# Twelve slots of a hand-written plan changed in a fused attention and feed-forward kernel: transposes of x at other places, held stores behind loads, the last tile by eight block products

## The chip, the cores and the metric

The kernel runs on one core of a Trainium2 chip. Its time is the device time of one launch in microseconds (us), as the median of several runs. A profiled execution gives a trace of every instruction on the core's engines: TensorE (PE, with its weight loads as PEld), VectorE (DVE), ScalarE (ACT), GpSimd (POOL) and SyncE (SP), and of its DMA queues. "Busy" is time in which an engine executes an instruction that the profile counts, and the "span" reaches from the first to the last event of the trace.

## The reference

Cosine-weighted linear attention for 8 batches of 8 heads, 576 rows and 64 columns each, followed by a feed-forward network over all 8 × 576 = 4608 rows of 512 columns:

```python
def phi(x, c, s):
    r = np.maximum(x, 0.0)
    return np.concatenate([r * c, r * s], axis=-1)
q_p, k_p = phi(q, cos_w, sin_w), phi(k, cos_w, sin_w)      # 64 -> 128 columns
kv  = np.einsum('bhsf,bhsd->bhfd', k_p, v)
z   = np.sum(k_p, axis=2)
num = np.einsum('bhsf,bhfd->bhsd', q_p, kv)
den = np.einsum('bhsf,bhf->bhs', q_p, z)[..., None] + 1e-06
x   = (num / den) -> rows (batch, s), columns (head, d)     # 4608 x 512
a, b = x @ w1, x @ w2                                       # 512 -> 1024 columns each
out = ((a * b) @ w3) @ w_out                                # 1024 -> 1024 -> 512
```

## The kernel before

**Tiles and stages.** The feed-forward part works on nine tiles `t` = 0 to 8 of 512 rows of x, the attention on eight batches `b` = 0 to 7, each cut into five chunks `c` = 0 to 4 of 128, 128, 128, 128 and 64 rows. Early on, w3 and w_out are multiplied into one matrix of 1024 × 512 (`w34b`), so that each tile needs x·w1, x·w2, their product element by element, and one more product with `w34b`. A chunk goes through these steps:

- `k`, `q` (features): the cosine half on VectorE (L494), the sine half on ScalarE (L498); a third number in the plan says how many heads ScalarE takes, and VectorE takes the others (L501). `v` copies a chunk of v beside a column of ones (L513 on GpSimd; `V` and `A` give it to VectorE or ScalarE).
- `qd`: a DMA transpose of a chunk's q features into `qpT`, issued by SyncE (L521). Some early chunks are transposed on TensorE instead (`qt`, and `xt` for x).
- `kv`: the products of all chunks of a batch on TensorE (L548), then two casts into `kvs`, on ScalarE (L552) and VectorE (L553).
- `n`: numerator and denominator of one chunk on TensorE (L580), eight products of `qpT` with `kvs`.
- `d`: the division on VectorE, three instructions (L591 to L593), which write `xblk`.
- `xd`: a DMA transpose of `xblk` into a place of the tile's `xT`, issued by SyncE (L613). There are three `xT` buffers in turn.

The rows of a batch fall into tiles of 512 so that tile 5 needs x of chunks 2, 3, 4 of batch 4 and 4, 0 of batch 5, tile 6 those of 1, 2, 3 of batch 5 and 0 of batch 6, tile 7 those of 1 to 4 of batch 6 and 4 of batch 7, and tile 8 those of 0 to 3 of batch 7. A numerator `n b c` reads 128 columns of `qpT`; for the short chunk 4, of 64 rows, it reads 64 columns of a neighbour as well, so that `n 5 1` reads what `qd 5 1` wrote, and `n 7 4` what `qd 7 4` and `qd 7 0` wrote.

**Order.** The order is written out by hand as a text, `PLAN` (L26 to L259). Each line is a slot and each step in it a call; the calls issue their instructions in this order, and every engine executes its own instructions in that order. `f t` takes the next piece of tile `t` (the generator `ffn_groups`, L658): four matmuls of a w1 product into a PSUM bank and the cast `asb` on ScalarE (L708), then four of a w2 product and the multiplication `abT` on VectorE (L714), eight times over, and then the products with `w34b`. There are four such PSUM banks (`ffn_pool`), and two more from `more` on, late in tile 7.

**Seven or eight block products.** For tiles in the tuple `SEVEN` the product with `w34b` is made from seven products of 256-column blocks (`seven_products`, L776, with the matmuls at L794), with sums of the operands on VectorE (`sums`, L774, called at L716 to L721) and additions of the results (`add`, L802). For the last tile it differs: GpSimd takes two of the additions (`ON_POOL`), the last product is made in two halves (L843), and `out_now` stores each block as soon as it is there, on SyncE and ScalarE. A tile that is not in `SEVEN` takes plain products (L729): three blocks of 128 rows with eight matmuls of 512 columns each, copied by ScalarE, and in the last tile stored by SyncE at once; the fourth block of the last tile in two halves of eight matmuls with 256 columns, copied by ScalarE and VectorE and each stored at once (L742 to L750).

**Loads and stores.** GpSimd's queue issues the loads of q, k and v: `l` at its place; `lg` behind a small copy (`gate`, L418) that reads the newest `asb`, so that the load starts no sooner; `lt` behind the same copy of the newest transposed column, that is, of the transpose which the plan issued last. The results of tiles 0 to 6 are held (`held`) in pairs of 128-row blocks, 512 KB each, until the plan stores the oldest pair: `st` by GpSimd, `sg` by GpSimd behind the newest `asb`, `sx` by GpSimd behind the newest transpose, `ss` by SyncE. `gx 0` does nothing at this place. There are twelve result buffers (`osbs`), so tiles 6 and 7 write where tiles 0 and 1 had theirs.

**What the profile's lines are.** Transposes on SyncE's queue show as `DMA_TRANSPOSE` of L521 (qpT<-qp) and L613 (xT<-xblk); loads on GpSimd's as `DMA_DIRECT2D` of L375 to L388; stores as `DMA_DIRECT2D` of L652.

The gates and the two forms of stores behind them, as far as the change uses them:

```python
def gate(behind):
    nc.gpsimd.tensor_copy(out=seen[0:behind.shape[0]], in_=behind)
...
def gated_store():                      # sg
    gate(newest[0][:, 0:1])
    store_next()

def store_behind_transposes():          # sx
    gate(transposed[0])
    store_next()
```

Of the kernel before, what the change touches and what calls it, by code (L numbers as in the profile page):

```python
# [89 lines left out]
f 1; d 2 4; lt 4 k 0; d 2 3  # L90
f 1; kv 3
f 2; tw 2
f 2; lg 4 q 0
f 2
f 2; l 4 q 1; qd 3 1
f 2
f 2; lt 4 v 1; n 3 0; qd 3 4
f 2
f 2; qd 3 2; tw 3
f 2  # L100
f 2
f 2; d 3 0
f 2; xd 2 4; n 3 1
f 2; q 4 0; q 4 4; d 3 1
f 2; q 4 3; v 4 4 V; l 4 k 1; xd 3 1; n 3 4
f 2
f 2; d 3 4
f 2; q 4 1 0
f 2; xd 2 3; xd 3 0; k 4 1; k 4 0; xd 3 4; qd 4 3; n 3 2
f 2; l 5 v 0  # L110
f 2
f 2; q 4 2
# [12 lines left out]
f 3  # L125
f 3; n 4 0; k 5 4; n 4 1; d 4 0; l 6 v 1
f 3; v 5 3 V
f 3; d 4 1; v 5 4 V; xd 3 2; qd 4 4; xd 4 0
f 3
f 3; n 4 2; k 5 1; xd 4 1  # L130
f 3
# [1 line left out]
f 3  # L133
f 3; q 5 0
f 3; d 4 2; lt 6 q 0; q 5 4
f 3; xd 3 3; k 5 0; n 4 3; v 6 4 V; xd 4 2
f 3
f 3; k 5 3 4; k 5 2; v 5 1 V; lg 6 k 0; q 5 3
f 4
f 3; lt 7 k 0; d 4 3  # L140
f 4; q 5 2; qd 5 0
f 4; n 4 4
f 4
f 4; q 5 1 6; d 4 4; qd 5 4; v 6 1 G
f 4
f 4; qd 5 2; l 6 q 1; kv 5; xd 4 3
f 4
f 4; n 5 0; v 6 0 G
f 4
f 4; d 5 0  # L150
f 4; n 5 4; qd 5 3
f 4; d 5 4
f 4
f 4; lt 6 k 1
f 4; k 6 4; qd 5 1
f 4; lg 7 k 1
f 4
f 4; xd 4 4; xd 5 0; lt 7 v 0
f 4; v 6 2 A
f 4; q 6 4  # L160
f 4; k 6 0 2; q 6 2; n 5 3; k 6 1 6; xd 5 4; q 6 0 4
f 4
f 5
f 4; d 5 3; n 5 1; k 6 3 2; q 6 3
# [2 lines left out]
f 5  # L167
f 5; v 6 3 V
f 5; d 5 1; k 6 2 0
f 5; l 7 q 0; st  # L170
f 5
f 5
f 5; kv 6; sg; k 7 3 6; lt 7 q 1; qd 6 2
f 5; n 5 2; k 7 2; k 7 1; k 7 0 4; lg 7 v 1; qd 6 0
f 5; qd 6 4; xd 5 3; qd 6 3
f 5
# [9 lines left out]
f 5; n 6 2  # L186
f 5
f 6; v 7 3 V; n 6 3
f 6; qd 6 1; d 6 2; q 7 2
f 6; st; xd 6 2; gx 0  # L190
f 6; q 7 4 2
f 6; k 7 4; q 7 0
f 6; v 7 4 V
f 6; n 6 1; v 7 1 V
f 6; d 6 1; q 7 3 2
f 6; qd 7 2
f 6; d 6 3; qd 7 4; q 7 1
f 6
f 6; qd 7 3
f 6; qd 7 0; sg  # L200
f 6; qd 7 1; kv 7
f 6; n 7 4; xd 6 1
f 6; d 7 4; xd 6 3
f 6; xd 7 4
f 6
f 6
f 6
f 6
f 6
# [47 lines left out]
f 8  # L257
f 8
f 8"""  # L259
SEVEN = (2, 3, 4, 5, 6, 7, 8)  # L260
ON_POOL = (8,)
NKP, NVA, NQP, NRQ, NRV, NT3 = 1, 2, 1, 2, 2, 3

# [50 lines left out]
def kernel(  # L314
# [343 lines left out]
    def ffn_groups(t):  # L658
# [38 lines left out]

        seven = t in SEVEN
        s = [fsb.tile([P, 4, 256], BF16, name=f"s{i}", bufs=1) for i in range(3)] if seven else None
# [277 lines left out]
```

## Time and profile before

| what | value |
|---|---|
| runs | 250.39, 246.68 and 248.56 us, median 248.56 |
| profiled execution: its own time | 247.64 us |
| its span | 245.9 us, 5417 instructions |
| granted TensorE clock | 0.999 over the span |
| TensorE busy | 233.7 us, 95%, 2024 matmuls in the records |
| VectorE busy | 196.4 us, 80% |
| ScalarE busy | 110.8 us, 45% |
| GpSimd busy | 82.4 us, 34% |
| loads and stores by software queues (q0) | 23.60 MB, 65.6% of the 16 DMA engines' span |
| transposes and SyncE's stores (q1) | 16.13 MB, 40.9% |
| first product of tile 5, 6, 7, 8 | 154.02, 177.4, 200.0 and 221.0 us |
| last store lands | 244.81 us |

The times of parts are those of the one profiled execution, counted from its span's start; its own time holds 1.7 us that lie outside the span. In a list of waits a row gives the engine, the tile and line of the waiting instruction, what it waited for, and then the sum of these waits, their number and the longest, in us. In a list of instructions a row gives the start, the length, the engine and line, the operation with its tiles and shapes, and in brackets how long the engine had been idle ahead of it and for whom.

### The profile page before, as it was taken

How to read it: one execution, taken by the hardware profiler on the slowest of the kernel's cores; microseconds unless marked ns; L12 is line 12 of the kernel's file. 1: busy time of each engine (PE TensorE's matmuls, PEld its weight loads, DVE VectorE, ACT ScalarE, POOL GpSimd, SP SyncE). 2: the span in 40 equal slices, each digit the busy share in tenths (PEclk: the TensorE clock that was granted, in tenths of full speed). 3: DMA queues.
4: the chain of work that ended last, by engine and by line, in shares of the span. 5: the costliest groups of instructions: out<-in, count | busy, mean ns of one | idle time of the engine just before them, and what ended most of it. 6: DMA issues, size and time to landing. Idle time of an engine off the chain costs nothing.

```text
span 245.9 us, 5417 instructions
## 1 busy us (share of the span) xinstructions
PE 233.7 (95%) x2024; PEld 145.6 (59%) x2051; DVE 196.4 (80%) x466; ACT 110.8 (45%) x196; POOL 82.4 (34%) x153
## 2 busy tenths in 40 slices
PE   8899999989999999999999997999999999999992
PEld 2589544566964544765585556555855675484481
DVE  6776577968979847999989989789999688785662
ACT  2743323767654833835484346337174302313320
POOL 8653987633504070007112311325000100083012
PEclk9999999999999999999999999999999999999999
DMA  6999999999999999999999997999855952599925
GB/s 192 193 196 199 190 180 194 199 199 174 130 186 132 178 150 178 172 129 152 185 119 133 176 173 89 129 209 242 109 77 104 188 42 43 109 281 329 271 84 171
DMA packets 85322, 40.47 MB, mean 165 GB/s; under 512 B 48048, under 2 KB 82864, under 8 KB 85296
## 3 DMA queue, kind: packets, MB, share of 16 engines
q0 software_dynamic: 37616, 23.60, 65.6%
q1 hardware_dynamic: 47264, 16.13, 40.9%
q10 hardware_dynamic: 416, 0.39, 0.5%
q8 instruction: 16, 0.26, 0.5%
q14 instruction: 10, 0.08, 0.1%
HBM read 38.80 MB, written 9.44 MB: 196 GB/s over the span
## 4 chain that ended last, share of the span: by engine, by line
PE 66%; DMA 15%; DVE 7%; POOL 6%; issue 3%; SPq 1%; ACT 0%; DVEq 0%; POOLq 0%
PE ffnps L667 40%; PE ffnps L794 12%; PE ffnps L729 5%; DMA w2b<-in_moe_w_dram 4%; PE pnum L580 4%; DMA kf<-in_k_dram 3%; POOL early L406 3%; DMA qpT<-qp 3%; PE ffnmore L794 2%; DMA q<-in_q_dram 2%; PE pnum L548 2%; DMA xT<-xblk 2%; DVE qp L494 1%; DVE abT L714 1%; POOL early L412 1%
## 5 line engine op out<-in xcount | busy, mean ns | idle before, releaser
L667 PE MATMUL ffnps<-xT,w1b 128*128 128x512 bf16 (+2 forms) x338 | 74.4, 338 | 2.9 <-DMA xT<-xblk 2.0
L667 PE MATMUL ffnps<-xT,w2b 128*128 128x512 bf16 (+2 forms) x346 | 75.2, 339 | 0.4
L708 ACT CAST asb<-ffnps 128x512 bf16<-128x512 f32 x64 | 37.5, 585 | 78.3 <-PE ffnps L667 62.2
L714 DVE TENSOR_TENSOR abT<-asb,ffnps 128x512 bf16<-128x512 bf16 x64 | 43.5, 682 | 17.3 <-PE ffnps L667 17.1
L667 PEld LDWEIGHTS <-w1b 128*128 128x128 bf16 x352 | 31.6, 98 | 30.0 <-issue 3.0
L667 PEld LDWEIGHTS <-w2b 128*128 128x128 bf16 x352 | 31.4, 98 | 26.8
L593 DVE TENSOR_TENSOR xblk<-pnum,den 128x512 bf16<-128x512 f32 (+1 forms) x39 | 26.9, 691 | 1.3
L794 PEld LDWEIGHTS <-abT 128*128 128x128 bf16 x224 | 21.6, 98 | 3.7
L498 ACT ACTIVATE kp<-kf,sinv 128x512 bf16<-128x512 bf16 (+4 forms) x33 | 20.5, 655 | 2.9 <-DMA kf<-in_k_dram 2.8
L498 ACT ACTIVATE qp<-qs,sinv 128x512 bf16<-128x512 bf16 (+6 forms) x30 | 18.4, 626 | 3.3 <-DMA qs<-in_q_dram 1.7
L580 PEld LDWEIGHTS <-qpT 128*128 128x128 bf16 x320 | 15.0, 98 | 7.5 <-issue 1.9
L418 POOL COPY seen<-xT 128x1 bf16<-128x1 bf16 x6 | 1.2, 194 | 48.3 <-DMA xT<-xblk 48.3
L580 PE MATMUL pnum<-kvs,qpT 128*128 128x65 bf16 x312 | 16.3, 194 | 1.0 <-DMA qpT<-qp 0.5
L418 POOL COPY seen<-asb 128x1 bf16<-128x1 bf16 x13 | 3.0, 233 | 41.5 <-ACT asb L708 41.5
L794 PEld LDWEIGHTS <-s 128*128 128x128 bf16 x160 | 15.5, 98 | 2.2
L729 PE MATMUL ffnps<-w34b,abT 128*128 128x512 bf16 x60 | 14.9, 379 | 0.2
L494 DVE TENSOR_SCALAR kp<-kf,cosv 128x512 bf16<-128x512 bf16 (+1 forms) x40 | 14.4, 378 | 0.3 <-DMA kf<-in_k_dram 0.3
L794 PE MATMUL ffnps<-w34b,abT 128*128 128x256 bf16 x112 | 14.5, 273 | 0.1
L473 PE MATMUL ffnps<-early,w3T 128*128 128x512 bf16 x62 | 14.2, 379 | 0.1
L513 POOL COPY va<-vs 128x512 bf16<-128x512 bf16 (+1 forms) x13 | 8.5, 667 | 15.2 <-DMA vs<-in_v_dram 15.2
L494 DVE TENSOR_SCALAR qp<-qs,cosv 128x512 bf16<-128x512 bf16 (+1 forms) x35 | 13.2, 383 | 0.0
L794 PE MATMUL ffnps<-early,s 128*128 128x256 bf16 x96 | 11.6, 273 | 0.0
(129 smaller groups left out, 323.7 us busy)
## 6 DMA issues: line engine op xcount, KB each, us to landing
kf<-in_k_dram POOLq DMA_DIRECT2D x7, 320.0 KB, 7.8
early<-in_moe_w_dram POOLq DMA_DIRECT2D x16, 128.0 KB, 5.2
out_dram<-osb SPq DMA_DIRECT2D x8, 256.0 KB, 3.6
qs<-in_q_dram POOLq DMA_DIRECT2D x6, 320.0 KB, 7.0
vs<-in_v_dram POOLq DMA_DIRECT2D x6, 320.0 KB, 9.1
kf<-in_k_dram POOLq DMA_DIRECT2D x7, 256.0 KB, 8.7
qs<-in_q_dram POOLq DMA_DIRECT2D x6, 256.0 KB, 8.4
vs<-in_v_dram POOLq DMA_DIRECT2D x6, 256.0 KB, 10.1
```

The costliest lines, as they stand in the source:

```text
L406: nc.gpsimd.dma_start(out=w3b[ts(a, 32), ds(g0, n), :].rearrange("p g (c j) -> p (g c) j", c=4), in_=moe_w3[ds(128 * g0, 128 * n), ts(a, 2 ...
L473: nc.tensor.matmul(acc[:, :], lhsT=w3T[:, lc, :], rhs=woutb[:, lc, :], start=(lc == 0), stop=(lc == 7))
L494: nc.vector.tensor_scalar(out=dst[:R, c, :, 0:D], in0=rows[:R], scalar1=0.0, scalar2=cosv[:R, at:at + 1], op0=ALU.max, op1=ALU.mult)
L498: nc.scalar.activation(out=dst[:R, c, 0:n, D:F], in_=rows[:R, 0:n], func=ACTF.Relu, scale=sinv[:R, at:at + 1], bias=0.0)
L513: (copy or nc.gpsimd.tensor_copy)(out=att_of(b)["va"][:R, c, :, 0:D], in_=raw[b, "v"][:R, :, c, :])
L580: nc.tensor.matmul(nt[:, h // 4, ds((h % 4) * 65, 65)], lhsT=qpT[:, h, ds(at, 128)], rhs=kvs[:, h, :], start=True, stop=True)
L593: nc.vector.tensor_tensor(out=xblk[rows, g0:g0 + ng], in0=n4[:, :, :, 0:D], in1=den[rows, 0:ng].unsqueeze(3).to_broadcast([R, ng, 4, D]), ...
L667: nc.tensor.matmul(out, lhsT=w[:, kc, ts(jc, 128)], rhs=x[:, kc, tok], start=(kc == 0), stop=(kc == 3))
L708: nc.scalar.copy(out=asb[:], in_=aT[:, :])
L714: nc.vector.tensor_mul(out=abT[:, jc, :], in0=asb[:], in1=bT[:, :])
L729: nc.tensor.matmul(ops[:, :], lhsT=abT[:, jc, ts(ms, 128)], rhs=w34b[:, jc, :], start=(jc == 0), stop=(jc == 7))
L794: nc.tensor.matmul(into[:, ts(ms, 256)], lhsT=a[:, kc, ts(ms, 128)], rhs=b[:, kc, :], start=(ms == 0 and kc == 0), stop=(ms == 1 and kc == 3))
```

## The change

Only the plan's text and the tuple `SEVEN` change; no function does. By place:

- **Tiles 2 and 3 (slots of `f 2` and `f 3`).** `xd 2 3` is issued ahead of `qd 3 1`, `qd 3 4` and `qd 3 2` instead of late in `f 2`; the steps `d 3 0`, `xd 3 0`, `n 3 1`, `d 3 1`, `xd 3 1`, `n 3 4`, `d 3 4`, `xd 3 4` and the features of batch 4 between them stand one to eight slots sooner. `xd 3 3` goes ahead of `xd 4 0`.
- **`f 4`.** `q 5 2`, `q 5 1` and `d 4 4` stand one to three slots later (`q 5 1` behind `kv 5`). `xd 4 4`, `xd 5 0` and `xd 5 4`, which were three in a row behind `qd 5 1`, go in between: SyncE's order `qd 5 2`, `xd 4 3`, `qd 5 3`, `qd 5 1`, `xd 4 4`, `xd 5 0`, `xd 5 4` becomes `qd 5 2`, `xd 4 3`, `xd 4 4`, `qd 5 3`, `xd 5 0`, `xd 5 4`, `qd 5 1`. As `lt` waits for the transpose issued last, `lt 6 k 1` now reads the x of `xd 5 0` instead of the q of `qd 5 3`, and `lt 7 v 0` and `lt 7 q 1` follow other transposes too.
- **`f 5` and `f 6`, stores.** The first four held pairs (tiles 0 and 1) were stored by `st` and `sg` in `f 5` and by `st` and `sg` in `f 6`. Now all four stand in `f 6`: `sg` behind the first and second of its `asb`, and near its end `sx` (behind `xd 7 4`) and `st`.
- **`f 6`, attention.** `d 6 3`, `xd 6 3`, `n 6 1`, `d 6 1`, `xd 6 1`, `qd 7 4`, `qd 7 0` and `kv 7` stand sooner. SyncE's order from `xd 6 2` on, `qd 7 2`, `qd 7 4`, `qd 7 3`, `qd 7 0`, `qd 7 1`, `xd 6 1`, `xd 6 3`, `xd 7 4`, becomes `qd 7 4`, `xd 6 3`, `qd 7 0`, `xd 6 1`, `qd 7 2`, `qd 7 3`, `qd 7 1`, `xd 7 4`.
- **Tile 8.** It leaves `SEVEN`, and so takes the plain products: three blocks and two halves of one. Its sums, additions and stores from `seven_products` go.

```diff
@@ -90,23 +90,23 @@
 f 1; d 2 4; lt 4 k 0; d 2 3
 f 1; kv 3
 f 2; tw 2
-f 2; lg 4 q 0
+f 2; xd 2 3; lg 4 q 0
 f 2
 f 2; l 4 q 1; qd 3 1
 f 2
 f 2; lt 4 v 1; n 3 0; qd 3 4
 f 2
 f 2; qd 3 2; tw 3
+f 2; d 3 0
+f 2; xd 3 0; n 3 1
+f 2; d 3 1
+f 2; xd 2 4; xd 3 1
+f 2; q 4 0; q 4 4; n 3 4
+f 2; q 4 3; v 4 4 V; l 4 k 1
 f 2
-f 2
-f 2; d 3 0
-f 2; xd 2 4; n 3 1
-f 2; q 4 0; q 4 4; d 3 1
-f 2; q 4 3; v 4 4 V; l 4 k 1; xd 3 1; n 3 4
-f 2
-f 2; d 3 4
+f 2; d 3 4; xd 3 4
 f 2; q 4 1 0
-f 2; xd 2 3; xd 3 0; k 4 1; k 4 0; xd 3 4; qd 4 3; n 3 2
+f 2; k 4 1; k 4 0; qd 4 3; n 3 2
 f 2; l 5 v 0
 f 2
 f 2; q 4 2
@@ -125,7 +125,7 @@
 f 3
 f 3; n 4 0; k 5 4; n 4 1; d 4 0; l 6 v 1
 f 3; v 5 3 V
-f 3; d 4 1; v 5 4 V; xd 3 2; qd 4 4; xd 4 0
+f 3; d 4 1; v 5 4 V; xd 3 2; qd 4 4; xd 3 3; xd 4 0
 f 3
 f 3; n 4 2; k 5 1; xd 4 1
 f 3
@@ -133,32 +133,32 @@
 f 3
 f 3; q 5 0
 f 3; d 4 2; lt 6 q 0; q 5 4
-f 3; xd 3 3; k 5 0; n 4 3; v 6 4 V; xd 4 2
+f 3; k 5 0; n 4 3; v 6 4 V; xd 4 2
 f 3
 f 3; k 5 3 4; k 5 2; v 5 1 V; lg 6 k 0; q 5 3
 f 4
 f 3; lt 7 k 0; d 4 3
-f 4; q 5 2; qd 5 0
+f 4; qd 5 0
 f 4; n 4 4
-f 4
-f 4; q 5 1 6; d 4 4; qd 5 4; v 6 1 G
-f 4
+f 4; q 5 2
+f 4; qd 5 4; v 6 1 G
+f 4; d 4 4
 f 4; qd 5 2; l 6 q 1; kv 5; xd 4 3
-f 4
+f 4; xd 4 4; q 5 1 6
 f 4; n 5 0; v 6 0 G
 f 4
 f 4; d 5 0
 f 4; n 5 4; qd 5 3
-f 4; d 5 4
+f 4; d 5 4; xd 5 0
 f 4
-f 4; lt 6 k 1
+f 4; lt 6 k 1; xd 5 4
 f 4; k 6 4; qd 5 1
 f 4; lg 7 k 1
 f 4
-f 4; xd 4 4; xd 5 0; lt 7 v 0
+f 4; lt 7 v 0
 f 4; v 6 2 A
 f 4; q 6 4
-f 4; k 6 0 2; q 6 2; n 5 3; k 6 1 6; xd 5 4; q 6 0 4
+f 4; k 6 0 2; q 6 2; n 5 3; k 6 1 6; q 6 0 4
 f 4
 f 5
 f 4; d 5 3; n 5 1; k 6 3 2; q 6 3
@@ -167,10 +167,10 @@
 f 5
 f 5; v 6 3 V
 f 5; d 5 1; k 6 2 0
-f 5; l 7 q 0; st
-f 5
-f 5
-f 5; kv 6; sg; k 7 3 6; lt 7 q 1; qd 6 2
+f 5; l 7 q 0
+f 5
+f 5
+f 5; kv 6; k 7 3 6; lt 7 q 1; qd 6 2
 f 5; n 5 2; k 7 2; k 7 1; k 7 0 4; lg 7 v 1; qd 6 0
 f 5; qd 6 4; xd 5 3; qd 6 3
 f 5
@@ -186,24 +186,24 @@
 f 5; n 6 2
 f 5
 f 6; v 7 3 V; n 6 3
-f 6; qd 6 1; d 6 2; q 7 2
-f 6; st; xd 6 2; gx 0
-f 6; q 7 4 2
-f 6; k 7 4; q 7 0
-f 6; v 7 4 V
-f 6; n 6 1; v 7 1 V
-f 6; d 6 1; q 7 3 2
+f 6; qd 6 1; d 6 2; q 7 2; sg
+f 6; xd 6 2; gx 0; q 7 4 2
+f 6; d 6 3; sg; q 7 0
+f 6; qd 7 4; k 7 4; xd 6 3
+f 6; n 6 1; v 7 4 V
+f 6; d 6 1; v 7 1 V; qd 7 0
+f 6; q 7 3 2; xd 6 1
 f 6; qd 7 2
-f 6; d 6 3; qd 7 4; q 7 1
+f 6; q 7 1
 f 6
-f 6; qd 7 3
-f 6; qd 7 0; sg
-f 6; qd 7 1; kv 7
-f 6; n 7 4; xd 6 1
-f 6; d 7 4; xd 6 3
-f 6; xd 7 4
+f 6; qd 7 3; kv 7
 f 6
+f 6; qd 7 1
+f 6; n 7 4
+f 6; d 7 4; xd 7 4
 f 6
+f 6; sx
+f 6; st
 f 6
 f 6
 f 6
@@ -257,7 +257,7 @@
 f 8
 f 8
 f 8"""
-SEVEN = (2, 3, 4, 5, 6, 7, 8)
+SEVEN = (2, 3, 4, 5, 6, 7)
 ON_POOL = (8,)
 NKP, NVA, NQP, NRQ, NRV, NT3 = 1, 2, 1, 2, 2, 3
 
```

## The prediction

> **What bounds the kernel now.** I read the page first, then the list of what TensorE waited for, then the chain of work in order of time, then the queues of SyncE and GpSimd around each wait.
>
> ```profile
> PE 233.7 (95%) x2024; PEld 145.6 (59%) x2051; DVE 196.4 (80%) x466; ACT 110.8 (45%) x196; POOL 82.4 (34%) x153
> ```
>
> TensorE is busy for 95% of the span of 245.9 us. A change of order can only take away its waits, and they are few. This is the whole list of them, each with its total, how often, and the longest:
>
> ```profile
> PE ffnps L667 <- DMA xT<-xblk: 2.0, 1, 2.0
> PE unread L456 <- DVE zeros L433: 1.2, 1, 1.2
> PE pnum L548 <- DVE kp L501: 0.6, 1, 0.6
> PE pnum L580 <- DMA qpT<-qp: 0.5, 1, 0.5
> PE kva L872 <- DVE kp L494: 0.5, 1, 0.5
> PE ffnps L667 <- DVE abT L714: 0.3, 1, 0.3
> PE kva L872 <- DMA vs<-in_v_dram: 0.3, 1, 0.3
> PE pnum L580 <- DVE kvs L553: 0.2, 1, 0.2
> ```
>
> L456 and L872 are the start, which the change doesn't touch. What it can reach are 2.0 (an x that is not yet transposed), 0.5 (a q that is not yet transposed), 0.3 and 0.2 (VectorE in `f 4`): 3.0 us in all, 1.2% of the time. To these comes the last tile, which is computed in another way.
>
> The 2.0 is the first product of `f 5`. The chain goes through one transpose on SyncE's queue:
>
> ```profile
> 148.22 5.66 DMA xT<-xblk
> 153.88 0.14 issue
> ```
>
> This is `xd 5 4`, the last of the x that `f 5` needs. SyncE's queue ahead of it, by runs of equal lines (start, length, count), and the landing times of the three x of the last run:
>
> ```profile
> 136.41 1.25 SPq L521 DMA_TRANSPOSE qpT<-qp  x1
> 137.71 2.33 SPq L613 DMA_TRANSPOSE xT<-xblk  x1
> 140.13 5.38 SPq L521 DMA_TRANSPOSE qpT<-qp  x2
> 145.61 3.81 SPq L613 DMA_TRANSPOSE xT<-xblk  x3
> ```
> ```profile
> DMA to landing us min/median/max: 2.3/5.7/6.2
> ```
>
> In order these are `qd 5 2`, `xd 4 3`, `qd 5 3`, `qd 5 1`, then `xd 4 4`, `xd 5 0`, `xd 5 4`. The first x of the run landed in 2.3 us, the other two in 5.7 and 6.2. Between them GpSimd sent a load:
>
> ```profile
> 146.30 0.19 POOL L418 COPY seen<-qpT 128x1 bf16<-128x1 bf16 x1 [8.96 <-DMA qpT<-qp]
> 146.75 0.68 POOL L375 DMA_DIRECT2D kf<-in_k_dram  x1 [0.26 <-issue]
> ```
>
> That is `lt 6 k 1`: a copy waits for the newest transpose of the plan (here `qd 5 3`), then the load goes out.
>
> **The x of `f 5` sooner (a gain of 1.3).** The same seven transposes now stand as `qd 5 2`, `xd 4 3`, `xd 4 4`, `qd 5 3`, `xd 5 0`, `xd 5 4`, `qd 5 1`. Nothing is added; `xd 5 4` is the sixth issue instead of the seventh, some 1.3 us sooner. More important, the copy of `lt 6 k 1` now waits for `xd 5 0`, so the load starts behind that one's landing and no longer in front of it. With 2.3 to 3 us per landing `xd 5 4` lands near 149.5, before TensorE asks for it, and the wait of 2.0 goes. What is late next is the load itself, by 0.4 us (were `xd 5 0` issued where the second of the pair stands now) to 1.7 (145.6 + 2.3 against the 146.2 of now). Who needs it is ScalarE:
>
> ```profile
> 151.57 0.40 ACT L498 ACTIVATE kp<-kf,sinv 128x128 bf16<-128x128 bf16 x1 [1.54 <-DMA kf<-in_k_dram]
> ...
> 153.00 0.49 ACT L498 ACTIVATE qp<-qs,sinv 128x256 bf16<-128x256 bf16 x1
> ```
> ```profile
> L708 ACT CAST asb<-ffnps 128x512 bf16<-128x512 f32 x64 | 37.5, 585 | 78.3 <-PE ffnps L667 62.2
> ```
>
> It sits idle for 1.54 us until the load is there, and has four activations to do before it comes to the copy `asb` that frees `f 5`'s first PSUM bank: 153.49 − 151.57 = 1.9, and 0.6 for that copy (585 ns on average, the group of L708). Today this is hidden behind TensorE's own wait. TensorE there:
>
> ```profile
> 150.98 1.04 PE L794 MATMUL ffnps<-early,abT 128*128 128x256 bf16 x8
> 154.02 1.02 PE L667 MATMUL ffnps<-xT,w1b 128*128 128x512 bf16 x3 [2.00 <-DMA xT<-xblk]
> ...
> 156.87 0.38 PE L667 MATMUL ffnps<-xT,w1b 128*128 128x512 bf16 x1
> ```
>
> From the first product of `f 5` to its second w1 product (156.87), which takes that bank again, TensorE has 2.9 us of work. Without the wait it is there at 152.0 + 2.9 − 0.3 (gains ahead of it) = 154.6. With the load landing at 152.0 to 153.3 the bank is free at 154.5 to 155.8: a new wait of 0 to 1.2. I take 0.7, the middle, so of 2.0 stay 1.3.
>
> `qd 5 1` pays for the turn: it is issued last, near 148.2, with the load behind it. `n 5 1` reads it just ahead of 153.5. With 3.2 us (the shortest rows for a q, below) it is in time, with 6.2 it is late by 0.9; that goes into the range.
>
> **VectorE in `f 4` (0.2).** `q 5 1` moves behind the cast `kvs` of `kv 5`, so the wait of 0.2 on `kvs` goes. The 0.3 on `abT` stays: its multiplication stands before everything that moves.
>
> **The q of batch 7 (0.6).** `n 7 4` waits for `qd 7 0`:
>
> ```profile
> 183.64 8.51 SPq L521 DMA_TRANSPOSE qpT<-qp  x5
> ```
> ```profile
> 189.44 3.21 DMA qpT<-qp
> 192.66 0.14 issue
> ```
>
> It is the fourth of these five now, and comes behind `qd 7 3`, whose features are made late. In the changed order it is the third from the same point (`qd 7 4`, `xd 6 3`, `qd 7 0`): 183.6 + 2 × 1.25 = 186.1, and 3.2 later it lands at 189.3, 2.6 before TensorE comes for it near 192. The 0.5 and the 0.14 of issue go: 0.6. On VectorE `d 6 3` moves ahead of two multiplications, but the sum of its work to `kv 7` is the same and a bank is asked for again only three to five products later; I cost it at 0 (upper bound 1.0, three instructions of one `d`).
>
> **The first held stores.** Two leave `f 5`, where TensorE has no wait that they could end. `f 6`, which had two, now has four; the first two stand right behind the copies of `asb` of its first two products:
>
> ```profile
> 178.48 0.59 ACT L708 CAST asb<-ffnps 128x512 bf16<-128x512 f32 x1 [5.20 <-DVE s L802]
> ```
> ```profile
> 180.00:184.00 4.00, 4.00 (x27) 1.99 (x26) 3.93 (x12) 2.73 (x6) 0.00 (x0) 1.00 0.69 80
> ```
>
> The window's last two numbers are the DMA share and 80 GB/s: there is room for 1 MB. But these are the microseconds in which the q of batch 7 are transposed. The one place of before where a store of half that size met them, with the landing times of the three q issued from 188.2 on:
>
> ```profile
> 190.50 1.04 POOL L652 DMA_DIRECT2D out_dram<-early  x2 [0.28 <-issue]
> ```
> ```profile
> DMA to landing us min/median/max: 3.2/3.2/7.6
> ```
>
> The q behind the store took 7.6, the two ahead of it 3.2. With 7.6 `qd 7 0` would land at 193.7, 1.7 late. I take 3.2 to 5, as the stores leave near 179.7 and 181.6, over 4 us ahead of it, where they met it by 0.4 here: cost 0, range 0 to 1.7. [...] The other two stores wait for `xd 7 4` and fall into `f 7`, without takers near.
>
> **The earlier moves (`xd 2 3` to `xd 3 4`, `xd 3 3`): 0.** No TensorE wait lies there. `xd 2 3` now stands ahead of three q of batch 3 and waits for `d 2 3`:
>
> ```profile
> 84.40 4.66 SPq L521 DMA_TRANSPOSE qpT<-qp  x3
> ```
> ```profile
> 84.87 0.69 DVE L593 TENSOR_TENSOR xblk<-pnum,den 128x512 bf16<-128x512 f32 x1
> ```
>
> So these go 1.2 + 1.25 = 2.4 us later, and with them the load `lt 4 v 1`, which waits for one of them. The loads ahead of it still run then; 0, with 1 us as upper bound.
>
> **The last tile (0.3).** Seven block products of 8 matmuls with 256 columns become eight: 24 with 512 columns and 16 with 256.
>
> ```profile
> 221.41 10.74 PE ffnps L667 x49
> ...
> 234.96 0.87 PE ffnps L794 x8
> ```
> ```profile
> 240.90 0.75 DVE L802 TENSOR_TENSOR osb<-ffnps,s 128x256 f32<-128x256 f32 x2
> ```
> ```profile
> DMA to landing us min/median/max: 2.2/2.8/3.1
> ```
>
> Per matmul 219 and 109 ns: 24 × 0.219 + 16 × 0.109 = 7.0 against 56 × 0.109 = 6.1, so TensorE ends 0.9 later. VectorE ends with one copy of 256 columns (0.4) instead of the two additions (0.75): 0.3 back. The stores decide more. Now all five of the tile, 1 MB, leave within the last 1.7 us, and the last of them takes 3.1. In the changed tile 256 KB leave behind each block of 1.75 us and 128 KB are last; I take 2.2, the shortest row, so 0.9 comes back. 0.9 − 0.3 − 0.9 = −0.3; bounds −0.5 and +0.6 (3.1 again). [...]
>
> **Sum.** 1.3 + 0.2 + 0.6 + 0.3 = 2.4. The profiled execution took 247.64 (its span and 1.7 around it), so 245.2 on its terms. The median of the runs shown is 248.56, 0.9 above it; a median should come to **246.2**.
>
> **The rivals.**
>
> *The wait changes its name (247.2).* The load of `lt 6 k 1` comes the full 1.7 late, or `qd 5 1` is late: of the 2.0 only 0.3 are gained, the sum is 1.4. For it: ScalarE's 1.54 of idling just there. Against: two transposes fewer ahead of the load.
>
> *Slower: the stores fill SyncE's queue (250.7).* Where transposes land late, the next issue is held: of the pair at 140.13 the run's 5.38 are 2.7 more than 2 × 1.3. If the two stores make transposes land in 7.6 and hold one issue ahead of `qd 7 0`, it lands at 186.1 + 2.7 + 7.6 = 196.4 and `n 7 4` waits 4.5 instead of 0.6: 3.9 lost against 1.8 gained elsewhere. It decides from a landing at 194.3 on. [...] Against: 80 GB/s in that window, and stores that left long before.
>
> *All waits go (244.7).* The load is in time (2.0), the 0.3 on `abT` goes too, 0.2, 0.6, and 0.8 from the tail: 3.9. Against: `abT` stands ahead of all that moves.
>
> **How the numbers follow.** Forecast 0.46, renamed wait 0.22, slower 0.17, all 0.15. The range from 243.6 to 250.8 takes in all cases and most of the spread of a median (the runs shown lie from 246.68 to 250.39). A difference of 2% (5 us) is about what a measurement of this kernel can tell from no change. Faster by that needs all waits gone and a favourable draw: 0.08. Slower by it needs two held issues, not one: 0.07. Within: 0.85.
>
> **What would show it.** In the changed profile: TensorE's list without the 2.0 on xT, and in its place up to 1 us on `asb` or on qpT near 154; the copy ahead of `lt 6 k 1` released by xT, not qpT; no wait at `n 7 4`; L843 gone, the last product near 240, the last store landing about 2.2 after its issue. I am wrong if the wait on xT stays, if a wait on qpT of over 2 us stands between 180 and 195, or if `f 7` starts with a wait on xT: `xd 7 4` keeps its place ahead of `f 7`.

## The result, and the profile after

| | before | after |
|---|---|---|
| median of all runs | 249.96 us (20 runs, 246.68 to 256.05) | 246.73 us (20 runs, 243.35 to 249.86) |
| ratio | | 0.9891, 95% interval 0.9862 to 0.9919 |
| profiled execution | 247.64 us, span 245.9 | 246.72 us, span 244.9 |

The change makes the kernel 1.1% faster, 2.7 us by the ratio; the forecast was 2.4 us, and 246.2. Ratios here and below leave out each kernel's slowest runs, while medians and counts are of all its runs. The two profiled executions differ by 0.9 us only: that of before was a lucky one, 2.3 under its median, and that of after was a typical one.

The head of the page after, and the list of what TensorE waited for (engine, tile, line, what for; the sum, the number, the longest):

```profile
PE 235.6 (96%) x2035; PEld 144.5 (59%) x2035; DVE 191.4 (78%) x455; ACT 111.7 (46%) x198; POOL 79.8 (33%) x152
```
```profile
PE ffnps L667 <- DMA xT<-xblk: 2.2, 1, 2.2
PE unread L456 <- DVE zeros L433: 1.2, 1, 1.2
PE pnum L580 <- DMA qpT<-qp: 1.1, 1, 1.1
PE kva L872 <- DVE kp L494: 0.8, 1, 0.8
PE pnum L548 <- DVE kp L501: 0.3, 1, 0.3
PE ffnps L667 <- DVE osb L802: 0.3, 1, 0.3
```

It reads almost like the list of before, with 2.2 for an x and 1.1 for a q. But neither stands where it stood. TensorE at the start of tile 5, and SyncE's queue ahead of it with the landing times of `xd 5 0` and `xd 5 4` (the run at 144.82):

```profile
152.08 1.03 PE L794 MATMUL ffnps<-early,abT 128*128 128x256 bf16 x8
152.95 1.03 PE L667 MATMUL ffnps<-xT,w1b 128*128 128x512 bf16 x4
```
```profile
144.82 2.88 SPq L613 DMA_TRANSPOSE xT<-xblk  x2
147.81 1.25 SPq L521 DMA_TRANSPOSE qpT<-qp  x1
```
```profile
DMA to landing us min/median/max: 2.3/2.4/2.5
```

The wait of 2.0 at tile 5 is gone, and the x land in 2.3 and 2.5 us instead of 5.7 and 6.2. The load of `lt 6 k 1` now leaves behind the landing of `xd 5 0`, and the load behind it (`lg 7 k 1`, at 148.86) behind that of `xd 5 4`:

```profile
147.40 0.19 POOL L418 COPY seen<-xT 128x1 bf16<-128x1 bf16 x1 [11.73 <-DMA xT<-xblk]
147.85 0.68 POOL L375 DMA_DIRECT2D kf<-in_k_dram  x1 [0.27 <-issue]
```

The 1.1 is new. It is `n 6 1`, waiting for `qd 6 1`; the rows are TensorE, GpSimd with the two stores that the change put there, and in the chain the transpose:

```profile
181.03 1.03 PE L667 MATMUL ffnps<-xT,w2b 128*128 128x512 bf16 x4
183.18 0.43 PE L580 MATMUL pnum<-kvs,qpT 128*128 128x65 bf16 x8 [1.11 <-DMA qpT<-qp]
```
```profile
178.45 0.57 POOL L652 DMA_DIRECT2D out_dram<-early  x1
180.22 0.19 POOL L418 COPY seen<-asb 128x1 bf16<-128x1 bf16 x1 [1.20 <-ACT asb L708]
180.73 0.55 POOL L652 DMA_DIRECT2D out_dram<-early  x1 [0.32 <-issue]
```
```profile
177.60 5.52 DMA qpT<-qp
183.13 0.05 issue
```

In before that transpose landed in 3.8 us and nobody waited for it. The 2.2 for an x is at the first product of tile 4, at 130.72, where `xd 4 1` landed 8.4 us after its issue. `n 7 4` waits for nothing. The tail from the first product of tile 8 to the last landing takes 23.4 us instead of 23.9.

So three things were open. Is the 2.2 at tile 4 the work of the change? Do the stores make the 1.1? And where do 2.7 us come from, when these two traces lie 0.9 apart?

### The profile page after: what moved, and what is told of

It is laid out like the page before. It is cut to its first block, busy times and chain, and to the rows that moved or that the text cites. A ratio compares the mean times of both kernels' runs of the same rounds, so it can differ in the third digit from the quotient of the medians.

```text
span 244.9 us, 5395 instructions
## 1 busy us (share of the span) xinstructions
PE 235.6 (96%) x2035; PEld 144.5 (59%) x2035; DVE 191.4 (78%) x455; ACT 111.7 (46%) x198; POOL 79.8 (33%) x152
## 4 chain that ended last, share of the span: by engine, by line
PE 81%; DVE 10%; DMA 6%; issue 1%; DVEq 0%; ACT 0%; ACTq 0%
PE ffnps L667 47%; PE ffnps L794 7%; PE ffnps L729 7%; PE unread L456 4%; PE ffnps L473 4%; DMA xT<-xblk 3%; PE pnum L548 3%; PE pnum L580 3%; DMA qpT<-qp 2%; PE ffnmore L794 1%; DVE xblk L593 1%; DVE kp L494 1%; PE pst L566 1%; DVE qp L494 1%; PE pst L620 1%
## 5 line engine op out<-in xcount | busy, mean ns | idle before, releaser
L667 PE MATMUL ffnps<-xT,w1b 128*128 128x512 bf16 (+2 forms) x352 | 76.0, 340 | 2.4 <-DMA xT<-xblk 2.2
L667 PE MATMUL ffnps<-xT,w2b 128*128 128x512 bf16 (+2 forms) x352 | 76.0, 340 | 0.0
L729 PE MATMUL ffnps<-w34b,abT 128*128 128x512 bf16 x88 | 20.8, 379 | 0.0
L794 PEld LDWEIGHTS <-abT 128*128 128x128 bf16 x192 | 18.5, 98 | 3.2
L794 PEld LDWEIGHTS <-s 128*128 128x128 bf16 x144 | 14.0, 98 | 2.0
L729 PEld LDWEIGHTS <-abT 128*128 128x128 bf16 x88 | 8.1, 98 | 8.5
L794 PE MATMUL ffnps<-w34b,abT 128*128 128x256 bf16 x96 | 12.4, 273 | 0.0
L494 DVE TENSOR_SCALAR qp<-qs,cosv 128x512 bf16<-128x512 bf16 (+1 forms) x35 | 11.9, 349 | 0.5 <-issue 0.5
```

Of the source, the lines that this page charges most:

```text
L494: nc.vector.tensor_scalar(out=dst[:R, c, :, 0:D], in0=rows[:R], scalar1=0.0, scalar2=cosv[:R, at:at + 1], op0=ALU.max, op1=ALU.mult)
L667: nc.tensor.matmul(out, lhsT=w[:, kc, ts(jc, 128)], rhs=x[:, kc, tok], start=(kc == 0), stop=(kc == 3))
L729: nc.tensor.matmul(ops[:, :], lhsT=abT[:, jc, ts(ms, 128)], rhs=w34b[:, jc, :], start=(jc == 0), stop=(jc == 7))
L794: nc.tensor.matmul(into[:, ts(ms, 256)], lhsT=a[:, kc, ts(ms, 128)], rhs=b[:, kc, :], start=(ms == 0 and kc == 0), stop=(ms == 1 and kc == 3))
```

## The experiments

**Both kernels once more.**

> The kernel before once more, for a second trace of it. Theory A (the waits of a trace belong to the kernel): TensorE waits 2.0 for x at the first product of tile 5, 0.5 to 0.7 for q at n 7 4, and not at the first product of tile 4; time ratio 1.00. Theory B (when transposes land beside loads is chance, and differs between executions by several us): the same order gives waits at other places and of other sizes, among them one at the first product of tile 4 in some executions, and the sum of waits behind 52 us differs from the 3.0 to 4 of the first trace by more than 1 us.

Measured: 250.79 us, ratio to itself 1.0055 (1.0012 to 1.0097). TensorE waits for x at tile 5 again, and idles 0.7 ahead of `n 7 4`; nothing over 0.4 at tile 4. This is the same kernel against itself, and the interval leaves out 1: half a percent between two kernels is not told apart by these runs, whatever their intervals say.

```profile
PE ffnps L667 <- DMA xT<-xblk: 2.6, 1, 2.6
```

The waits at tile 5 and `n 7 4` belong to the kernel. But the span is 3.5 us longer than that of the first trace. Some 1.1 of that are lost before the wait at tile 5 begins, and 0.6 in the wait. Most of the rest is in the windows behind it (length, busy time of PE, PEld, DVE, ACT and POOL; last the granted clock, the DMA share, GB/s):

```profile
148.00:152.00 4.00, 4.00 (x42) 3.59 (x41) 3.57 (x8) 2.35 (x5) 1.58 (x3) 1.00 0.85 97
152.00:156.00 4.00, 1.40 (x18) 0.94 (x15) 3.59 (x11) 1.92 (x4) 1.18 (x3) 0.95 0.64 80
156.00:158.00 2.00, 2.00 (x7) 0.88 (x6) 0.00 (x0) 0.34 (x1) 1.36 (x2) 0.50 0.92 108
158.00:160.00 2.00, 2.00 (x19) 1.30 (x17) 0.72 (x2) 1.15 (x3) 0.00 (x0) 0.75 1.18 135
160.00:164.00 4.00, 4.00 (x20) 1.84 (x19) 3.76 (x11) 1.17 (x2) 0.00 (x0) 1.00 1.39 175
```

Right behind the wait the granted clock is 0.50, and it is back at 1.00 by 160: 0.5 × 2 + 0.25 × 2 + 0.05 × 4 = 1.7 us lost, that no list of waits shows. By the same numbers the low stretch reaches from 155.6 to 159.0. From tile 5's first product to `n 5 1` TensorE takes 3.3 us here and 1.7 in the first trace of before, where the same stretch had 1.00 throughout:

```profile
156.00:158.00 2.00, 2.00 (x16) 0.94 (x13) 1.93 (x5) 0.64 (x2) 0.01 (x1) 1.00 1.04 99
158.00:160.00 2.00, 2.00 (x11) 0.93 (x10) 2.00 (x6) 0.81 (x2) 0.00 (x0) 1.00 1.33 180
```

> The changed kernel once more, for a second trace. Theory A: the wait of 2.2 for x at the first product of tile 4 and that of 1.1 for q at n 6 1 are there again, within 0.5; ratio 0.989. Theory B: at least one of the two is gone or differs by over 1 us, while tile 5 again starts without a wait; ratio 0.989.

Measured: 247.38 us, ratio 0.9914 (0.9878 to 0.9950). No wait for x anywhere in the list; `n 6 1` still waits:

```profile
PE pnum L580 <- DMA qpT<-qp: 0.4, 1, 0.4
```

So the wait at tile 4 came and went with the execution (theory B), the one at `n 6 1` stayed, smaller.

**xd 3 3 at its old place.** Changed kernel, with

```diff
-f 3; d 4 1; v 5 4 V; xd 3 2; qd 4 4; xd 3 3; xd 4 0
+f 3; d 4 1; v 5 4 V; xd 3 2; qd 4 4; xd 4 0
...
-f 3; k 5 0; n 4 3; v 6 4 V; xd 4 2
+f 3; xd 3 3; k 5 0; n 4 3; v 6 4 V; xd 4 2
```

> The changed kernel with xd 3 3 back at its place of before, behind xd 4 1. Theory A (xd 3 3 ahead of xd 4 0 makes the last x of tile 4 late): the wait of 2.2 at the first product of tile 4 goes, tile 4 starts about 2 us sooner, ratio to before 0.981. Theory B (the five transposes and the loads share the DMA engines, and their sum lands at the same time in any order): tile 4 starts within 0.7 us of the changed kernel's time on average, ratio 0.987 to 0.991.

Measured: 0.9872 (0.9809 to 0.9935), which does not tell it from the changed kernel's two ratios. Tile 4 starts with an idle 0.1, as it does with 0 to 0.5 in every trace of either order but one. So the 2.2 comes in one execution and not in the next; that `xd 3 3` has no part in it is not shown. With it ahead, `xd 4 1` landed in 5.9 to 8.4 us (four traces), with it behind in 5.3 to 6.0 (ten). This trace has a wait that the others lack: `n 3 1` waits 2.2, because `qd 3 1` landed in 10.4 us.

**The last tile alone.** Before with `SEVEN = (2, 3, 4, 5, 6, 7)`.

> The kernel before with the last tile by eight block products and nothing else changed. From the first product of tile 8 to the last landing of a store 23.4 us instead of 23.9 (the changed kernel's trace has 23.4): ratio 0.998. If the tail does more than the trace shows (a store of the last five late in other executions): 0.994 or less. If it does nothing: 1.000.

Measured: 1.0001 (0.9959 to 1.0044). The traces show what the timed runs don't: from tile 8's first weight load to the last landing it is 23.4 us here and in the seven other traces with the changed last tile, and 23.9 in six with the old one. That is half a microsecond, less than the runs resolve.

**The order in f 4 alone.** Before, with the diff's hunk between `f 4; q 5 2; qd 5 0` and `f 4; k 6 0 2; ...`.

> The kernel before with only the part in f 4 changed (xd 4 4, xd 5 0, xd 5 4 ahead of qd 5 1; q 5 1, q 5 2, d 4 4 later). Theory A (this part takes away the wait for the x of tile 5, 2.2 to 2.8 in three traces of before, and what follows it on asb is 0 to 1.5): xd 5 0 and xd 5 4 land in 2.3 to 2.5 us, no wait for x at tile 5, n 7 4 still waits 0.7; ratio 0.992. Rival (the wait changes its name): a wait of 1.5 to 2 on asb or on the q of qd 5 1 in tile 5; ratio 0.998.

Measured: median 254.94 us (247.01 to 260.16), slower than before's 249.40; the ratio of 0.9987 (0.9936 to 1.0039) rests on 4 of the 10 runs. In the trace, which is of the run of 260.16, the x land in 2.3 and 2.5 and tile 5 starts on time. Then, 20 us later, TensorE stands at `n 6 0` and `n 6 4`:

```profile
174.61 0.43 PE L580 MATMUL pnum<-kvs,qpT 128*128 128x65 bf16 x8 [1.49 <-DMA qpT<-qp]
...
183.57 0.60 PE L580 MATMUL pnum<-kvs,qpT 128*128 128x65 bf16 x8 [5.91 <-DMA qpT<-qp]
```
```profile
DMA to landing us min/median/max: 8.8/14.4/15.6
```

The last row is the landing of four q of batch 6 (shortest, median, longest). In before they landed in 3.1 to 10.4. The wait moved to a place that neither the forecast nor my expectation named. The four runs of 247.0 to 249.7 cannot have had all of it, so how long it is differs between executions. The clock was at 0.50 behind it:

```profile
183.00:185.00 2.00, 1.43 (x13) 1.16 (x14) 0.00 (x0) 0.00 (x0) 0.00 (x0) 0.50 1.20 265
185.00:187.00 2.00, 2.00 (x12) 1.37 (x10) 1.02 (x3) 0.00 (x0) 0.00 (x0) 0.50 0.01 0
```

**The stores back in f 5.** Changed kernel, with

```diff
-f 5; l 7 q 0
+f 5; l 7 q 0; st
...
-f 5; kv 6; k 7 3 6; lt 7 q 1; qd 6 2
+f 5; kv 6; sg; k 7 3 6; lt 7 q 1; qd 6 2
```

and in `f 6` the stores `sg`, `sg`, `sx`, `st` replaced by `st` ahead of `xd 6 2` and `sg` behind `qd 7 1`.

> The changed kernel with the held stores about where before had them: st and sg in f 5, st and sg in f 6, the latter behind qd 7 1. Theory A (the two stores early in f 6 make qd 6 1 land in 4.8 to 5.5 us instead of 3.3 to 3.8): qd 6 1 lands in 3.3 to 3.9, the wait at n 6 1 (0.55 to 1.3 in three traces) goes; ratio 0.985 to 0.988. Rival (n 6 1 waits because it stands a slot sooner): 0.5 or more stays at n 6 1; ratio 0.989 to 0.991.

Measured: median 255.47, ratio 1.0131 (1.0029 to 1.0232; 2 of 4 runs), the opposite of both. `qd 6 1` does land in 3.5 us and `n 6 1` doesn't wait, as theory A has it. But the q of batch 6 land in 8.4 to 11.7, and `n 6 4` pays, in a trace of the fastest run (250.89):

```profile
176.42 0.60 PE L580 MATMUL pnum<-kvs,qpT 128*128 128x65 bf16 x8 [3.04 <-DMA qpT<-qp]
```

**f 4 and the stores together.** Before, with the `f 4` hunk and the change's move of the stores, nothing else.

> The kernel before with two parts of the change: the order in f 4 and the stores moved to f 6; tiles 2 and 3, the attention of f 6 and the last tile as before. Theory A (without the store's and the load's bytes beside the q of batch 6, qd 6 3 lands before n 6 4 asks, so that the gain at tile 5 is kept): no wait at n 6 0 and n 6 4, where the f 4 order alone had 1.65 and 6.1; ratio 0.988 to 0.993, clocks mostly 0.997 or more. Rival (the f 4 order moves the wait to batch 6 whatever the stores do): a wait of 1.5 or more at n 6 4, ratio 0.997 or more.

Measured: 247.55 us, 0.9919 (0.9883 to 0.9956), no wait at `n 6 0` or `n 6 4`. The order in `f 4` shows no gain without the stores' move, and the two together bring the gain, as far as these runs can tell it from the changed kernel's. The stores' move alone was not run. What is left at tile 5 is the renamed wait of the forecast, on the copy by ScalarE:

```profile
PE ffnps L667 <- ACT asb L708: 1.3, 1, 1.3
```

**The load behind the x.** Before with `lt 6 k 1` moved from its slot to behind `xd 5 4`. The features of `k 6 0` and `k 6 1` then stand ahead of the load and take half of their rows from what the buffer held, so they don't wait for it.

> The kernel before, SyncE's order unchanged, with only lt 6 k 1 moved behind xd 5 4, so that its gate waits for xd 5 4 and no load runs beside xd 5 0 and xd 5 4. Theory A (it is the load that makes these two land in 5.7 to 7 us): they land in 2.3 to 3, the wait for x at tile 5 goes to 0.3 or less, and ScalarE's features of batch 6 come late in its place: a wait of 2 to 4 on asb in tile 5; ratio 0.998 to 1.006. Rival (it is the place in SyncE's queue, seventh instead of sixth): they still land in 5 to 7 us and the wait of over 2 stays.

Measured: 253.14 us, 1.0103 (1.0047 to 1.0158). The next load in GpSimd's queue (`lg 7 k 1`) moved up and ran beside the x instead, so that they landed in 5.3 and 5.0 us, and tile 5 starts 1.0 late instead of 2.0: the run doesn't separate the loads from the place in the queue. The traces do for the sixth place: the x there took 6.2 us in before, with both loads sent, and 2.3 in after, with the first load sent 1.0 ahead of its landing. The other half of the expectation shows, and larger: the load comes late for the features that need it, and TensorE waits 7.2 us on `asb`, where 2 to 4 were expected.

**The moves in f 2 and f 3 undone.** Changed kernel with the first hunk and `xd 3 3` as in before.

> The changed kernel with the moves in f 2 and f 3 undone (xd 2 3 to xd 3 4, and xd 3 3, as in before). Theory A (these moves cost: qd 3 1 lands in 6.1 to 10.4 us behind xd 2 3 instead of 3.4 to 4.5, and tile 4's x come late in some executions): qd 3 1 lands within 5 us, no wait at n 3 1, at most 0.4 at tile 4; tile 3 starts 0.3 to 0.7 later for xd 3 4 in some executions; ratio 0.985 to 0.988. Rival (they bring what the traces don't show): ratio 0.992 or more.

Measured: 0.9888 (0.9835 to 0.9942), the changed kernel's ratio. `qd 3 1` lands in 3.4 us instead of 5.1 to 10.4 in the five traces of the new order, but it has the time in all of them but one.

**TensorE kept busy through its wait.** Before, with work that the product behind it overwrites:

```diff
             aT = ffn_tile()
+            if t == 5 and jc == 0:
+                for _ in range(8):
+                    nc.tensor.matmul(aT[:, :], lhsT=w1b[:, 0, 0:128], rhs=w2b[:, 0, 0:512], start=True, stop=True)
```

> The kernel before with eight more matmuls of 512 columns (1.75 us, on weights that are there, into the bank of tile 5's first product, which overwrites them) ahead of that product: TensorE works through most of its wait for x instead of idling. x lands when it did, so tile 5 starts when it did. Theory A (an idle stretch of TensorE of about 2.4 us or more lets the granted clock fall to half for some 3.5 us; traces: idle 2.47 to 3.21 with 0.50 behind it, 2.16 and 2.32 without): the idle time at tile 5 is 0.4 to 1.2, the clock stays 1.00 between 155 and 165, and the median of the runs falls by 1 to 2 us; ratio 0.993 to 0.997. Rival (the clock falls by itself, whatever TensorE does): the runs are as slow as before's, ratio 0.999 to 1.003, with clocks of 0.99 as often.

Measured: 248.23 us against 249.64 of before on the same chip; ratio 0.9973 (0.9934 to 1.0011), between the two expectations, and the interval reaches 1. Tile 5 starts at 153.95 as in the first trace (154.02), with 0.7 of idling left ahead of it, and the clock behind it stays:

```profile
156.00:158.00 2.00, 2.00 (x14) 0.92 (x11) 1.93 (x5) 0.64 (x2) 0.00 (x0) 1.00 1.05 122
158.00:160.00 2.00, 2.00 (x11) 0.88 (x9) 2.00 (x6) 0.81 (x2) 0.00 (x0) 1.00 1.35 186
```

One run of 12 has a mean clock under 0.995; of before it is 15 of 29 on this chip and 46 of 88 in all (its runs beside the experiments), with a median of 250.3 against 248.5 of the others. So it is the idling that makes the clock fall: with work that brings nothing in its place, the fall is rare. What that saves is less sure, 1.4 us by the medians and 0.7 by the ratio.

**Two attempts to take the 1.1 away.** First, the changed kernel without the moves in `f 2` and `f 3` and with the two stores later: `sg`, `sg` out, and `sx`, `st` behind `qd 7 0`.

> The changed kernel with the moves in f 2 and f 3 undone, and with the two stores early in f 6 put behind the landing of qd 7 0 (sx, st). Theory A (those stores are what makes qd 6 1 late): qd 6 1 lands in 3.3 to 3.9 us, no wait at n 6 1, nothing new at n 7 4; 1.0 us sooner than the changed kernel, ratio to before 0.983 to 0.987. Rival (the stores meet the q of batch 7 there, or tile 6's outputs wait for them): a wait of 1 us or more at n 7 3, n 7 2 or at tile 6's first block product, ratio 0.989 or more.

Measured: 251.16 us, above before's 249.64; the ratio of 0.9945 (0.9894 to 0.9996) rests on 4 of the 12 runs, and the other eight have a mean clock of 0.991 to 0.993. In the trace `qd 6 1` lands in 3.1 us and `n 6 1` doesn't wait, but the rival holds: tile 6 writes its results where tile 0's stood, and ScalarE waits 4.49 for their store, TensorE 2.8 for ScalarE. The q behind the two stores, `qd 7 3` and `qd 7 1`, land in 9.7 and 8.9 us instead of 3.3 and 3.1, which nobody waits for.

```profile
199.19 0.59 ACT L816 COPY early<-ffnps 128x512 f32<-128x512 f32 x1 [4.49 <-DMA out_dram<-early]
```

Second, the changed kernel with `n 6 1` two slots later and the stores left:

```diff
-f 6; n 6 1; v 7 4 V
-f 6; d 6 1; v 7 1 V; qd 7 0
-f 6; q 7 3 2; xd 6 1
-f 6; qd 7 2
-f 6; q 7 1
+f 6; v 7 4 V
+f 6; v 7 1 V; qd 7 0
+f 6; n 6 1; q 7 3 2
+f 6; d 6 1; qd 7 2
+f 6; xd 6 1; q 7 1
```

> The changed kernel with n 6 1 two slots later, d 6 1 and xd 6 1 behind it, stores as in the changed kernel. Theory A (qd 6 1 lands 6.0 to 6.8 us behind the start of tile 6 beside the stores, and TensorE comes for it 5.4 behind it, now 7.2): the wait at n 6 1 of 0.55 to 1.3 goes, n 7 4 still doesn't wait; ratio to before 0.984 to 0.988. Rival (what is taken from n 6 1 comes back at kv 7 or n 7 4, which share its PSUM banks and VectorE): a wait of 0.5 or more there, ratio 0.989 to 0.992.

Measured: 246.89 us against 249.82, 0.9877 (0.9831 to 0.9923). No wait for a q is left in the list, and nothing came in its place at `kv 7` or `n 7 4`; tile 6 takes 22.0 us instead of 23.3 and 22.5. What it gains over the changed kernel, 0.4 to 0.9 us by the ratios, is less than their intervals.

## Why the prediction was right, point by point

- **The x of tile 5 (1.3 forecast).** Right in its mechanism: `xd 5 4` was forecast to land near 149.5 and landed at 148.8. It was two loads, though, and not one that stood between the x in before: behind `lt 6 k 1` (146.75) the gate also holds `lg 7 k 1` (147.77), and the x are late with the second alone (5.3 and 5.0 us in the run with the load behind the x). Three traces of before waited 2.0, 2.6 and 2.3 there; none of the nine with the new order did. The renamed wait on `asb`, taken as 0.7, was 1.3, 0.8, 1.1, 1.3, 0.3, 1.3 and three times nothing: 0.7 on average. `qd 5 1` took 5.4 to 6.9 us, and `n 5 1` did not wait.
- **That wait's price** is the step that was too low: "of 2.0 stay 1.3" counts the idle time alone. In half of before's runs the mean clock is under 0.995; in the second trace of before and in that with the last tile alone the fall stands right behind this wait, and costs 1.7 us. Runs with a clock of 0.995 or more have medians of 248.5 before (42 of 88) and 246.7 after (25 of 32): 1.8 us apart. The other 1.1 of the 2.9 between the medians of all these runs, 249.7 and 246.8, goes with the low clock having become rarer, 7 of 32 runs instead of 46 of 88.
- **VectorE in `f 4` (0.2).** The wait on `kvs` is in neither trace of after; the one on `abT` in `f 4` is missing in one and 0.5 in the other. Small, as forecast.
- **The q of batch 7 (0.6).** `qd 7 0` landed at 188.84, forecast 189.3; `n 7 4` waits in no trace with this order.
- **The first held stores (0).** This step failed twice. "Two leave `f 5`, where TensorE has no wait that they could end" holds for before, not for the changed order: with tile 5 on time, those stores cost 3 us at `n 6 4` in the trace with the stores back. They are three pairs and not two: the plain `st` of `f 6` in before waits for nothing and leaves at 168.0, in tile 5. And in `f 6` I weighed them against `qd 7 0`, which they don't reach; they meet `qd 6 1`, 0.8 us ahead of the first of them, which lands in 5.5 instead of 3.8 us. That `n 6 1` also comes a slot sooner is the other half: two slots later it waits no more.
- **The earlier moves (0).** Right: undone, the ratio is the same.
- **The last tile (0.3).** 0.5. The landing of the last 128 KB was taken as 2.2, the shortest row of before, and measured 1.9; the last issue came 0.7 later, forecast 0.6.
- **The rivals.** "The wait changes its name" came true for 0.7, as the forecast had it. "The stores fill SyncE's queue" did not happen at `qd 7 0`, but its mechanism, stores that make q late, is what the kernel with the `f 4` order alone shows, one tile earlier: the q of batch 6 land in 8.8 to 15.6 us there and in 7.6 to 12.0 with the stores moved.
- **The sum.** 2.4 forecast; 2.7 by the ratio. Terms too high and too low offset one another: the clock (1.1) was missing on the one side, `n 6 1` (0.4 to 1.1) on the other. That the time of 246.2 came so near 246.73 is luck: it started from 248.56, a median of three runs that 20 runs put at 249.96, and from there the same sum gives 247.6.

## What to carry to other kernels

A wait that ends moves everything behind it sooner, and with it the reserves that hid other transfers: here the order in `f 4` was worth nothing until the stores left the tile behind it. Before pricing a wait, look at the granted clock in the windows right behind it, in more than one execution; here a wait of 2.6 us on TensorE cost 4.3 in one execution, with the clock at 0.50 behind it, and one of 2.0 only its length in another, with the clock at 1.00. And a profile is one draw: this one was 2.3 us better than the median, in good part because it was spared the fall of the clock that half of the other runs had.

## What the runs showed of the hardware

**A clock that falls behind a short wait.** Nine waits of TensorE of 2.0 us or more lie in these traces. At six (2.2, 2.3, 2.6, 3.0, 5.9 and 7.2 us) the granted clock went to 0.50; at three (2.0, 2.2 and 2.8) it stayed 1.00. No length divides the two: a wait of 2.2 lies on either side. The five traces without such a wait have a mean clock of 0.996 or more.

By the windows, worked out as for the second trace of before, the low stretch is 3.4 us long at the waits of 2.2, 2.3, 2.6 and 3.0, and 6.8 and 10.2 at those of 5.9 and 7.2. In the 3.4 us ahead of the fall TensorE idled 2.1 us in the wait of 7.2, 2.4 in that of 2.6, 2.8 in that of 3.0, and all 3.4 in that of 5.9. But the 2.8 in one piece in the first of the two attempts brought no fall. So what divides the six from the three is not shown, and no run moved a wait on purpose.

**Transposes beside loads.** The x chunks of tile 5 land in 2.3 to 2.5 us alone (2.3 and 2.5 in after) and in 5.0 to 7.0 beside one or two loads of k (5.7 and 6.2 in before); the q of `qd 5 1` in 3.2 to 3.3 alone (3.2 in before) and 5.4 to 6.9 beside the same two loads (5.6 in after); the four q of batch 6, in the kernel with the `f 4` order alone and with four loads and three stored pairs beside them in its plan, in 8.8 to 15.6.
